# Strassen chunks of a fused attention and MoE kernel: four queues of small work rearranged (q loads, norms' spread, block 2's weights, weight sums)

## The chip, the cores and the metric

The kernel runs on one core of a Trainium2 chip. The metric is device microseconds of one execution. A core has TensorE (PE, matrix products into PSUM banks), VectorE (DVE), ScalarE (ACT), GpSimd (POOL) and SyncE (SP), each with an instruction queue of its own that runs in order. A DMA is issued from one of these queues, and an instruction that waits for a semaphore holds up all that stands behind it in its queue.

## What is computed

```python
def _attn_ref(q, k, v, g_norm):                # 8 batches, 8 heads, 576 rows, 64 columns
    kv = np.einsum('bhsd,bhse->bhde', k, v)
    out = np.einsum('bhsd,bhde->bhse', q, kv)
    rms = np.sqrt(np.mean(out * out, axis=-1, keepdims=True) + 1e-06)
    return (out / rms * g_norm).astype(np.float32)

def _moe_ref(x, w_in, w_out):                  # x 4608 x 512, d_ff 2048
    h = x @ w_in
    g = np.maximum(0.01 * h, h)
    return (g @ w_out).astype(np.float32)

def _moe2_ref(x, w_in, w_out, a, b):
    h = x @ w_in
    h2 = h * h
    h3 = h2 * h
    P = a[0] + a[1] * h + a[2] * h2 + a[3] * h3
    Q = 1.0 + np.abs(b[0]) * np.abs(h) + np.abs(b[1]) * h2
    g = P / (Q + 1e-06)
    return (g @ w_out).astype(np.float32)
```

The output of attention, with the heads side by side, goes through `_moe_ref` (block 1) and then `_moe2_ref` (block 2).

## The kernel before

**Tiling.** The 4608 tokens are nine chunks of 512. d_ff is 16 blocks of 128. Each product of block 1 and block 2 is three products of float16 parts (high x high, high x low, low x high; lines 432 to 434, `mm3`). Block 1 is a loop over units. Chunks 0 to 3 are computed in the classical way, a slot for each of the 16 blocks of d_ff. Chunks 4 to 8 (units 6 to 10 of the loop at L1193) use Strassen's seven products for h = x w_in, on 128 x 256 pieces: each of eight steps `j` covers two blocks of d_ff, hence slots 2j and 2j + 1, and 16 slots a chunk again.

**A step j** (L1245 to L1283). `product` fills two PSUM banks in turn, `chain` and `other`. What is in `chain` is copied to the tile `hq` by ACT (L1253, L1261, L1271, L1277), what is in `other` is added to it by DVE (L1255, L1273, L1278). The next product for a bank waits until that is done. Between the products stand `y_steps`, the matmuls y += g w_out of earlier blocks. `split_g` (L1039) is called once a step: Prelu on ACT, the high part of g by an ACT copy (L301), the low part by a DVE subtraction (`split_lo`, L296).

**The other work** of a slot is put between these by hand-set places and by queues. `prep(c, ...)` (from L888) gives the pieces that make the next chunk's x, each with a slot and a place in it ("load", "early", "pe", "post"):

- `ldq` loads q (L568, four DMAs of 64 x 2 x 512) and `mo` multiplies it by kv into the banks `po`;
- `so` scales `po` into `o` (L916 on DVE for chunks above 3, else ACT), `sq` squares `po` on ACT (L909);
- `ms` sums the squares in PSUM (`pm`), `nm` makes the reciprocal norms `w` (L612 to L621);
- `store_w` writes `w` to DRAM (`rs`, L935, SP), and `load_w` calls `spread_w` twice (L715): two DMAs that read `rs` back, broadcast over partitions, into `sq`, one on SP's queue and one on ACT's;
- `sx` multiplies `o` by the spread norms (L946, DVE), and `sf` makes the forms of x that Strassen needs (L515, L523, L525);
- the `bursts` load the k and v tiles of a later batch (L560, SP).

Block 2's w_in and w_out arrive as 64-bit floats, in 32 halves, and are converted to float32 on the way: `convert2` (L1060) asks for a half (L311) on ACT's queue with two raw tiles in turn, `next_half` puts ACT's absolute value (L320), four DVE steps (L325, L327, L331, L335) and a maximum (`top`, L158 and L1090) on the queue `fill`, and one slot later the half is stored to DRAM (L1065), on ACT's queue too. One converted tile `cv` of two parts is used in turn. Strassen's sums of block 1's weights are made in unit 5, the last classical chunk: `sums_w(j)` on DVE (L398, L403) every second slot, `forms_w(j, 0)` on ACT (L410), `forms_w(j, 1)` on DVE (L296).

`begin(sl)` and `end(sl)` add the pieces of a slot to the queue `work`; `drain(vector, scalar)` takes pieces from `evacs`, `work` and `fill`, in this order, as long as their own costs (DVE us, ACT us) fit the two budgets:

```python
while evacs or work or fill:
    for q in (evacs, work, fill):
        if q and q[0][0] <= vector and q[0][1] <= scalar and (q[0][0] + q[0][1] or first):
            v, a, fn = q.pop(0)
            break
```

What is asked for at a place stands at that place in the engine's queue; a queue of DMAs (SP's above all) runs ahead of the others as far as its waits allow.

## Time and profile before

| | us |
|---|---|
| median of 3 runs | 1591.68 |
| lowest and highest run | 1590.59, 1593.63 |
| the profiled execution | 1589.82 |
| its span | 1588.0 |
| the five Strassen chunks in it, 383.71 to 826.54 | 442.83 |

All numbers of the trace come from the one profiled execution. In a view of waits each row gives the engine and line that waited, what it waited for, the sum, the number of times and the longest. In a timeline each row gives the start, the duration, the engine and line, the operation with its output and inputs, and in square brackets the idle time of the engine just before it with what ended it. A row of SPq or ACTq is a DMA being issued by that queue, not the transfer.

### The profile page before, as it was taken

The page shows a single profiled execution, that of the slowest core. Times are in us where ns is not written, and L with a number is a line of the kernel's source. Part 1 is how long each engine was busy: PE and PEld are TensorE (multiplying, and loading weights), DVE is VectorE, ACT ScalarE, POOL GpSimd, SP SyncE. Part 2 cuts the span into 40 slices and gives each one's busy share as a digit, 9 for nine tenths or more (in the row PEclk, how much of TensorE's full clock was granted, in tenths as well). Part 3 has the DMA queues.
Part 4 walks back from the last instruction along what each step waited for, and adds up shares of the span by engine and source line. Part 5 has one row for each costly group of instructions (what it writes and reads, how often), then busy time and mean ns, then how long its engine had stood idle before and what let it go on. Part 6 is the DMA issues. An engine that isn't in the chain of part 4 may idle for free.

```text
span 1588.0 us, 21127 instructions
## 1 busy us (share of the span) xinstructions
PE 1557.0 (98%) x8634; PEld 851.4 (54%) x8634; DVE 1112.7 (70%) x1491; ACT 930.8 (59%) x1277; POOL 150.1 (9%) x74
## 2 busy tenths in 40 slices
PE   9999999999999999989999999999999999999998
PEld 5888754444666665656654444444444444444444
DVE  6787456679566565656658767777777777777776
ACT  6567554444454443544567665766666666666665
POOL 0000000000000000000001221222221222211221
PEclk9999999999999999999999999999999999999999
DMA  8454632252454424240241010101010100101000
GB/s 316 124 190 142 171 107 67 69 144 60 137 129 140 127 87 119 80 154 19 89 138 54 1 54 2 54 1 53 1 53 1 35 19 9 45 0 53 1 27 27
DMA packets 44069, 123.07 MB, mean 77 GB/s; under 512 B 4804, under 2 KB 5188, under 8 KB 43972
## 3 DMA queue, kind: packets, MB, share of 16 engines
q1 hardware_dynamic: 32432, 92.23, 18.0%
q10 hardware_dynamic: 11540, 29.50, 6.5%
q8 instruction: 67, 1.10, 0.3%
q14 instruction: 30, 0.25, 0.1%
HBM read 90.25 MB, written 31.46 MB: 77 GB/s over the span
## 4 chain that ended last, share of the span: by engine, by line
PE 89%; DVE 4%; ACT 3%; DMA 3%; issue 1%; ACTq 0%; SPq 0%; DVEq 0%
PE y L432 15%; PE y L434 15%; PE y L433 15%; PE ph L432 11%; PE ph L434 11%; PE ph L433 11%; PE chain L432 2%; PE chain L434 2%; PE chain L433 2%; PE other L432 1%; PE other L434 1%; PE other L433 1%; DMA raw<-in_kv_dram 1%; PE kvacc L578 1%; PE po L595 1%
## 5 line engine op out<-in xcount | busy, mean ns | idle before, releaser
L296 POOL TENSOR_TENSOR g<-p,g 128x1024 f16<-128x1024 f32 x70 | 149.9, 2142 | 1414.2 <-ACT g L301 1397.7
L1297 ACT ACTIVATE e<-ph,small 128x1024 f32<-128x1024 f32 (+1 forms) x73 | 80.4, 1101 | 237.0 <-PE ph L434 237.0
L432 PE MATMUL ph<-x,v 128*128 128x512 f16 x576 | 218.3, 379 | 0.5 <-DVE hq L1278 0.5
L434 PE MATMUL y<-g,v 128*128 128x512 f16 x576 | 218.3, 379 | 0.3 <-POOL g L296 0.3
L433 PE MATMUL ph<-x,v 128*128 128x512 f16 x576 | 218.3, 379 | 0.0
L434 PE MATMUL ph<-x,v 128*128 128x512 f16 x576 | 218.3, 379 | 0.0
L433 PE MATMUL y<-g,v 128*128 128x512 f16 x576 | 218.3, 379 | 0.0
L432 PE MATMUL y<-g,v 128*128 128x512 f16 x576 | 218.3, 379 | 0.0
L1300 DVE SCALAR_TENSOR_TENSOR e<-s,b,e 128x1024 f32<-128x1024 f32 (+1 forms) x73 | 92.7, 1270 | 148.9 <-ACT s L1298 148.9
L432 PEld LDWEIGHTS <-v 128*128 128x128 f16 x1152 | 112.7, 98 | 137.0 <-DVE hq L1278 0.8
L434 PEld LDWEIGHTS <-v 128*128 128x128 f16 x1152 | 112.7, 98 | 136.0
L433 PEld LDWEIGHTS <-v 128*128 128x128 f16 x1152 | 112.7, 98 | 135.7
L433 PE MATMUL y<-g,n 128*128 128x512 f16 x448 | 171.1, 382 | 0.0
L432 PE MATMUL y<-g,n 128*128 128x512 f16 x448 | 171.0, 382 | 0.0
L434 PE MATMUL y<-g,n 128*128 128x512 f16 x448 | 170.9, 381 | 0.0
L434 PEld LDWEIGHTS <-n 128*128 128x128 f16 x816 | 80.1, 98 | 71.6 <-issue 1.4
L433 PEld LDWEIGHTS <-n 128*128 128x128 f16 x816 | 80.0, 98 | 70.4 <-issue 14.3
L432 PEld LDWEIGHTS <-n 128*128 128x128 f16 x816 | 80.1, 98 | 64.1 <-issue 7.2
L1308 DVE SCALAR_TENSOR_TENSOR e<-e,z 128x1024 f32<-128x1024 f32 (+1 forms) x73 | 88.6, 1214 | 29.1 <-ACT z L1305 29.0
L1307 DVE SCALAR_TENSOR_TENSOR p<-p,small,ph 128x1024 f32<-128x1024 f32 (+1 forms) x73 | 92.5, 1266 | 2.6
L1309 DVE SCALAR_TENSOR_TENSOR p<-p,small,z 128x1024 f32<-128x1024 f32 (+1 forms) x73 | 92.2, 1264 | 0.0
L1310 DVE SCALAR_TENSOR_TENSOR p<-e,p 128x1024 f32<-128x1024 f32 (+1 forms) x73 | 88.4, 1210 | 2.5
(219 smaller groups left out, 2882.0 us busy)
## 6 DMA issues: line engine op xcount, KB each, us to landing
raw<-in_kv_dram SPq DMA_DIRECT2D x33, 512.0 KB, 5.7
tmp<-in_w_dram SPq DMA_DIRECT2D x32, 512.0 KB, 7.0
w<-in_w_dram ACTq DMA_DIRECT2D x32, 512.0 KB, 4.5
raw<-x SPq DMA_DIRECT2D x18, 512.0 KB, 5.2
w<-cv ACTq DMA_DIRECT2D x32, 256.0 KB, 2.4
raw<-w SPq DMA_DIRECT2D x16, 512.0 KB, 4.2
out_dram<-raw SPq DMA_DIRECT2D x16, 512.0 KB, 2.9
raw<-in_qT_dram SPq DMA_DIRECT2D x28, 256.0 KB, 8.6
```

The source lines that it names most:

```text
L296: (nc.gpsimd if pool else nc.vector).tensor_tensor(out=lo, in0=src, in1=hi if hi.dtype == F16 else hi.bitcast(F32), op=ALU.subtract)
L432: nc.tensor.matmul(out=dst, lhsT=wl, rhs=xh, start=first, stop=False, **kw)
L433: nc.tensor.matmul(out=dst, lhsT=wh, rhs=xh, start=False, stop=False, **kw)
L434: nc.tensor.matmul(out=dst, lhsT=wh, rhs=xl, start=False, stop=last, **kw)
L578: nc.tensor.matmul(out=acc[s * D:(s + 1) * D, k * D:(k + 1) * D], lhsT=t[:, 0, c], rhs=t[:, 1, c], start=first and k == 0, stop=last, skip ...
L595: nc.tensor.matmul(out=dst[s][j * D:(j + 1) * D, o], lhsT=KV[bt][r, 2 * g + j, :], rhs=q[r, j, o], start=True, stop=True)
L1297: nc.scalar.activation(out=e, in_=ph, func=AF.Abs, scale=k["e"])
L1300: nc.vector.scalar_tensor_tensor(out=e, in0=s, scalar=b1[:, 0:1], in1=e, op0=ALU.mult, op1=ALU.add)
L1307: nc.vector.scalar_tensor_tensor(out=p, in0=p, scalar=k["c1"], in1=ph, op0=ALU.add, op1=ALU.mult)
L1308: nc.vector.scalar_tensor_tensor(out=e, in0=e, scalar=Q_C, in1=z, op0=ALU.add, op1=ALU.mult)
L1309: nc.vector.scalar_tensor_tensor(out=p, in0=p, scalar=k["c0"], in1=z, op0=ALU.add, op1=ALU.mult)
L1310: nc.vector.scalar_tensor_tensor(out=p, in0=e, scalar=-2.0, in1=p, op0=ALU.add, op1=ALU.mult)
```

## The change

Seven edits, all in the loop over block 1's units:

1. `spread_w`: for chunks from 4 on, both halves of the norms' spread are issued on SP's queue.
2. For chunks 5 to 7 `prep` asks for the q of the chunk after its own (`ldq_next`) in its slot 6, where before each chunk asked for its q in slot 0 of the unit that prepares it.
3. `so` is done by ACT for all chunks.
4. `store_w` and `load_w` are put at the place "early" of their slots for chunks above 4, and kv tiles 3 and 4 get places of their own.
5. Block 2's weights are loaded and stored by GpSimd's queue; a half is stored at once in `top`, which also asks for another; nothing is asked for in slots 7 and 8 of a chunk, and in the last two of these units up to four halves are on the way, in tiles of the pool `raw`.
6. `sums_w` and `forms_w` start two slots earlier, in slot 14 of unit 4, and are done in slot 14 of unit 5. In unit 5 `drain` is called only in slots 0 to 8.
7. The low part of `split_g` is put on a queue `urgent`, which `drain` looks at after `evacs`, and the budget of the drain at the end of an even slot is 4.2 in place of 3.0.

```diff
-                (nc.sync, nc.scalar)[j].dma_start(out=t[j * D:(j + 1) * D], in_=rs[c].rearrange("(p r) n -> r p n", r=32)[j:j + 1]
+                (nc.scalar if c < 4 and j else nc.sync).dma_start(out=t[j * D:(j + 1) * D], in_=rs[c].rearrange("(p r) n -> r p n", r=32)[j:j + 1]
...
-                    st["q", g] = load_q(c, g)
+                    st["q", g] = made.pop(("q", c, g)) if ("q", c, g) in made else load_q(c, g)
+                def ldq_next(g):
+                    made["q", c + 1, g] = load_q(c + 1, g)
...
-                    if c > 3:
-                        nc.vector.tensor_scalar_mul(st["o"][:, p, :], ps, gsc[:, 0:1])
-                    else:
-                        nc.scalar.activation(out=st["o"][:, p, :], in_=ps, func=AF.Copy, scale=gsc[:, 0:1])
+                    nc.scalar.activation(out=st["o"][:, p, :], in_=ps, func=AF.Copy, scale=gsc[:, 0:1])
...
+                    if 4 < c < NCH - 1:
+                        at(6, "load", ldq_next, g)
...
-                at(ms_at + 1, "post", store_w)
-                at(w_at, "pe", load_w)
+                at(ms_at + 1, "early" if c > 4 else "post", store_w)
+                at(w_at, "early" if c > 4 else "pe", load_w)
...
-                split(*(x.rearrange("p a (b n) -> p (a b) n", b=2) for x in gt), hq)
+                hi, lo = (x.rearrange("p a (b n) -> p (a b) n", b=2) for x in gt)
+                nc.scalar.activation(out=hi, in_=hq, func=AF.Copy)
+                urgent.append((1.23, 0, lambda: split_lo(hi, lo, hq)))
...
-                while made["late"] and made["late"][0][0] <= count["slot"]:
-                    _, dst, t = made["late"].pop(0)
-                    nc.scalar.dma_start(out=dst, in_=t)
-                n = count["asked"]
-                if n < 2 * NF and n - count["done"] < 2:
-                    t = wp.tile([P, N], I64, tag=made["raw"][n % 2], name="w64")
-                    made[n] = load_w64(w2, *halves[n], t, nc.scalar), count["slot"] + 2
+                ask()
+                next_half()
+
+            def ask():
+                n, deep = count["asked"], 4 if count["slot"] > 48 else 2
+                if n < 2 * NF and n - count["done"] < deep and count["slot"] % NF not in (7, 8):
+                    t = raw(1, I64)[:, 0, :] if deep > 2 else wp.tile([P, N], I64, tag=made["raw"][n % 2], name="w64")
+                    made[n] = load_w64(w2, *halves[n], t, nc.gpsimd), count["slot"] + 2
                     count["asked"] += 1
...
-                    made["late"].append((count["slot"] + 1, w2f[f][:, part, :], u()[:, 0, :].bitcast(F32)))
+                    nc.gpsimd.dma_start(out=w2f[f][:, part, :], in_=u()[:, 0, :].bitcast(F32))
                     count["done"] += 1
+                    ask()
...
-                    for q in (evacs, work, fill):
+                    for q in (evacs, urgent, work, fill):
...
+                    if ui == 4 and sl > 13 or ui == 5 and sl < NF - 1:
+                        n = sl + 2 if ui > 4 else sl - 14
+                        if n % 2:
+                            forms_w(n // 2, 0)
+                        else:
+                            if n > 1:
+                                forms_w(n // 2 - 1, 1)
+                            if n < NF:
+                                sums_w(n // 2)
                     if ui == 5:
-                        if sl % 2 == 0:
-                            sums_w(sl // 2)
-                            if sl > 0:
-                                forms_w(sl // 2 - 1, 1)
-                        else:
-                            forms_w(sl // 2, 0)
                         convert2()
-                        drain(1.4, 0.7)
+                        if sl < 9:
+                            drain(1.4, 0.7)
...
-            forms_w(NP - 1, 1)
...
-                                 [(5, 6, c + 2, (0, 1, 2)), (7, 8, c + 2, (3, 4))] if c + 2 < B else [],
+                                 [(5, 6, c + 2, (0, 1, 2)), (5, 8, c + 2, (3,)), (8, 9, c + 2, (4,))] if c + 2 < B else [],
...
-                    drain(3.0, 2.1)
+                    drain(4.2, 2.1)
```

Three pieces of the engines' queues show what this moves. The first is DVE's queue where the Strassen chunks begin, before: `sum` and `s` are the weight sums, `cv` a half of block 2's weights, `g` the low part of g.

```order
L398 TENSOR_TENSOR sum_3376<-n_2578 128x512
L398 TENSOR_TENSOR sum_3376<-n_2617 128x512
L403 TENSOR_TENSOR sum_3376<-sum_3376 128x256 x4
L296 TENSOR_TENSOR s_3347<-sum_3300,s_3347 128x4x256
L325 TENSOR_SCALAR cv<-cv 128x512
L327 TENSOR_SCALAR cv<-cv 128x512
L296 TENSOR_TENSOR g_3371<-t,g_3371 128x512
L331 SCALAR_TENSOR_TENSOR cv<-w_3259,cv 128x512
L335 SCALAR_TENSOR_TENSOR cv<-w_3259,cv 128x512
L296 TENSOR_TENSOR s_3407<-sum_3376,s_3407 128x4x256
L1255 TENSOR_TENSOR hq<-hq,other 128x256
```

The same place in the changed kernel, up to its first addition into `hq` (L1255 is now L1262):

```order
L523 SCALAR_TENSOR_TENSOR x16T_4_3322<-sq,small,x16T_4_3322 128x512
L296 TENSOR_TENSOR g_3283<-t,g_3283 128x512
L523 SCALAR_TENSOR_TENSOR x16T_4_3326<-sq,small,x16T_4_3326 128x512
L523 SCALAR_TENSOR_TENSOR x16T_4_3361<-sq,small,x16T_4_3361 128x512
L523 SCALAR_TENSOR_TENSOR x16T_4_3363<-sq,small,x16T_4_3363 128x512
L296 TENSOR_TENSOR g_3367<-t,g_3367 128x512
L296 TENSOR_TENSOR s_3345<-sum_3301,s_3345 128x4x256
L296 TENSOR_TENSOR g_3367<-t,g_3367 128x512
L1262 TENSOR_TENSOR hq<-hq,other 128x256
```

The sums are gone from here, and so are their conversions by ACT from the rows ahead of ACT's first copy. The second place is SP's queue while the second Strassen chunk is prepared in the first (`rs_91` holds its norms, `raw<-in_qT_dram` is q, `raw<-in_kv_dram` k and v):

```order
 L560 DMA raw<-in_kv_dram 128x1024 x4
+L568 DMA raw<-in_qT_dram 64x2x512 x4
 L560 DMA raw<-in_kv_dram 64x1024
 L935 DMA rs_91<-w 128x512
-L715 DMA sq<-rs_91 64x4x512
-L568 DMA raw<-in_qT_dram 64x2x512 x4
+L715 DMA sq<-rs_91 64x4x512 x2
```

The q loads now stand ahead of the norms' store instead of behind the spread, and the second half of the spread has come from ACT's queue. The third place is POOL's queue around the first two of these chunks, which had no such rows before (`w_3_98` and its like are block 2's weights in DRAM, `w_3895` and its like the raw tiles):

```order
L1095 DMA w_2_97<-cv 128x512
L1095 DMA w_3_98<-cv 128x512
L311 DMA w_3895<-in_w_dram 128x512
L311 DMA w_3938<-in_w_dram 128x512
L1095 DMA w_3_98<-cv 128x512
L311 DMA w_4044<-in_w_dram 128x512
```

Two loads stand there directly behind one store, where elsewhere a store and a load take turns.

## Rows read from the trace of the kernel before

**Rows 1.** The page's first part: engine, busy us, share of the span, instructions.
```profile
PE 1557.0 (98%) x8634; PEld 851.4 (54%) x8634; DVE 1112.7 (70%) x1491; ACT 930.8 (59%) x1277; POOL 150.1 (9%) x74
```

**Rows 2.** PE's waits in the Strassen chunks: total us, times, longest.
```profile
PE other L432 <- DVE hq L1278: 8.7, 6, 4.5
PE chain L432 <- ACT hq L1253: 6.6, 3, 2.5
PE other L432 <- DVE hq L1273: 3.6, 4, 0.9
PE other L432 <- DVE hq L1255: 2.0, 4, 1.3
PE chain L432 <- ACT hq L1271: 0.9, 4, 0.3
```

**Rows 3.** Stretches: us, engines' busy us, PE's granted clock, DMA share, GB/s.
```profile
383.71:826.54 442.83, 419.84 (x2949) 267.76 (x2947) 278.52 (x506) 214.60 (x370) 0.00 (x0) 0.99 0.37 112
388.93:392.34 3.41, 2.72 (x9) 1.28 (x9) 3.34 (x7) 0.64 (x3) 0.00 (x0) 0.50 0.00 0
627.86:631.27 3.41, 3.41 (x13) 1.67 (x12) 3.41 (x6) 1.64 (x3) 0.00 (x0) 0.50 0.01 2
```

**Rows 4.** Timeline at the start of the first Strassen chunk (place A).
```profile
387.88 1.06 ACT L410 ACTIVATE s<-sum 128x1024 f16<-128x1024 f32 x1 [2.62 <-DVE sum L403]
...
389.25 0.37 PE L432 MATMUL chain<-x16T,s 128*128 128x256 f16 x1 [2.49 <-ACT hq L1253]
...
393.23 0.27 PE L432 MATMUL other<-x16T,s 128*128 128x256 f16 x1 [1.26 <-DVE hq L1255]
```

**Rows 5.** Timeline in the second Strassen chunk (place B).
```profile
495.92 0.75 DVE L916 TENSOR_SCALAR o<-po,gsc 128x512 f32<-128x512 f32 x1
496.70 0.60 ACT L909 ACTIVATE sq<-po 128x512 f32<-128x512 f32 x1 [0.66 <-DVE o L916]
497.19 0.66 ACT L320 ACTIVATE cv<-w 128x512 f32<-128x512 f32 x1
...
497.88 0.43 DVE L325 TENSOR_SCALAR cv<-cv 128x512 f32<-128x512 f32 x1 [1.22 <-ACT cv L320]
...
498.81 0.69 DVE L331 SCALAR_TENSOR_TENSOR cv<-w,cv 128x512 uint32<-128x512 uint32 x1
...
499.88 0.27 PE L432 MATMUL other<-x16B,s 128*128 128x256 f16 x1 [0.90 <-DVE hq L1273]
```

**Rows 6.** Timeline in the first Strassen chunk (place C).
```profile
433.61 1.54 SPq L935 DMA_DIRECT2D rs<-w  x1
...
438.75 0.66 ACT L320 ACTIVATE cv<-w 128x512 f32<-128x512 f32 x1 [3.67 <-DMA rs<-w]
...
439.73 0.27 PE L432 MATMUL chain<-x16T,s 128*128 128x256 f16 x1 [1.77 <-ACT hq L1253]
```

**Rows 7.** Timeline in the third and fourth Strassen chunk (place D).
```profile
611.52 3.42 SPq L568 DMA_DIRECT2D raw<-in_qT_dram  x4
...
612.95 0.65 ACTq L715 DMA_DIRECT2D sq<-rs  x1
...
625.45 0.69 DVE L946 TENSOR_TENSOR o<-o,sq 128x512 f32<-128x512 f32 x1 [5.43 <-DMA w<-cv]
...
626.53 0.27 PE L432 MATMUL other<-x16B,n 128*128 128x256 f16 x1 [3.46 <-DVE hq L1278]
...
715.14 0.69 DVE L946 TENSOR_TENSOR o<-o,sq 128x512 f32<-128x512 f32 x1 [6.50 <-DMA w<-in_w_dram]
```

**Rows 8.** Timeline, first chunk; then landings of spread (520 to 540), norms' store, weight loads.
```profile
448.07 0.69 DVE L946 TENSOR_TENSOR o<-o,sq 128x512 f32<-128x512 f32 x1 [1.66 <-DMA sq<-rs]
...
DMA to landing us min/median/max: 6.0/7.3/8.6
...
DMA to landing us min/median/max: 2.0/3.2/4.3
...
DMA to landing us min/median/max: 4.0/4.6/9.4
```

More of the change, by code (lines that the diff above doesn't have):

```diff
@@ L963, in prep @@
                     at(po_at[g], "pe", mo, g)
+                    if 4 < c < NCH - 1:
+                        at(6, "load", ldq_next, g)
                     for p in (2 * g, 2 * g + 1):
-                        at(po_at[g] + 1, "early", so, p, cost=(0.75, 0) if c > 3 else (0, 0.7))
+                        at(po_at[g] + 1, "early", so, p, cost=(0, 0.7))
                         at(po_at[g] + 1, "early", sq, p, cost=(0, 0.6))
@@ L1000 @@
             k1 = 7
-            steps, work, fill, evacs = [], [], [], []
+            steps, work, fill, evacs, urgent = [], [], [], [], []
             def y_steps(n):
@@ L1062, in convert2 @@
                 count["slot"] += 1
-                while made["late"] and made["late"][0][0] <= count["slot"]:
-                    _, dst, t = made["late"].pop(0)
-                    nc.scalar.dma_start(out=dst, in_=t)
-                n = count["asked"]
-                if n < 2 * NF and n - count["done"] < 2:
-                    t = wp.tile([P, N], I64, tag=made["raw"][n % 2], name="w64")
-                    made[n] = load_w64(w2, *halves[n], t, nc.scalar), count["slot"] + 2
+                ask()
[5 more added lines that the diff above has]
+                    made[n] = load_w64(w2, *halves[n], t, nc.gpsimd), count["slot"] + 2
                     count["asked"] += 1
-                next_half()
             def next_half():
@@ L1102, in drain @@
                 next_half()
-                while evacs or work or fill:
-                    for q in (evacs, work, fill):
+                while evacs or urgent or work or fill:
+                    for q in (evacs, urgent, work, fill):
                         if q and q[0][0] <= vector and q[0][1] <= scalar and (q[0][0] + q[0][1] or first):
@@ L1124 @@
                 elif ui == 5:
-                    made["late"] = []
                     made["cv"], *made["raw"] = (room.pop(0) for _ in range(3))
@@ L1204 @@
                     room.extend(spare_q + [made["cv"]] + made["raw"])
-                    assert count["done"] == 2 * NF and not made["late"]
+                    assert count["done"] == 2 * NF
                 def chores(sl):
@@ L1281 @@
                     r = hq, c, j
+                    assert not urgent
                 while work:
@@ L1284 @@
             split_g(r)
+            urgent.pop()[2]()
             assert not steps
```

## The prediction

> **What bounds the kernel now.** The page comes first: TensorE (PE) is busy 98% of the span [rows 1]. VectorE (DVE, 70%), ScalarE (ACT, 59%) and GpSimd (POOL, 9%) cost nothing but where PE waits for them. The profiled execution is 1589.82 us, of which 1588.0 are span and 1.82 lie outside it; the median of the runs is 1591.68, that is 1.86 longer, and a saving is taken off both alike.
>
> The change touches the Strassen chunks, so the view by stretches comes next: the five chunks take 442.83 us, PE is busy in 419.84 of them, and 22.99 are idle [rows 3]. The view of waits names them [rows 2]: nearly all is PE waiting until a `hq` operation has emptied one of two PSUM banks, `chain` (by ACT copies) or `other` (by DVE additions). So every gap is a late ACT or DVE instruction, and the question for each is what stood ahead of it in its queue. The timeline answers that at four kinds of place, which I call A to D.
>
> A third loss hides in busy time. After the gap of A and after both gaps of D, PE's clock is granted at 0.50, the level of 1.2 GHz, for 3.41 us [rows 3], where the third dip would read as the second. Work done at half the clock takes twice as long: 2.72/2 + 3.41/2 + 3.41/2 = 4.77 us lost. The idle times ahead were 2.49, 3.46 and 4.53; after the idle times of 1.77 and 2.35 at C the clock stayed up.
>
> **The change part by part.**
>
> *Place A, start of the first Strassen chunk (weight sums two slots earlier).* ACT's conversion of the last weight sum waits 2.62 us for DVE's sums, the first copy out of `chain` stands behind it in ACT's queue, and PE waits 2.49. A second later sum then stands ahead of DVE's first addition, 1.26 [rows 4]. In the new order both sums are done in the chunk before, and the first rows of either queue in this chunk are the copies and additions themselves. Gain 2.49 + 1.26 = 3.75, and the dip behind it, 1.36. The sums now lie beside the classical chunks, where DVE did the same work before and PE shows no wait for it; I cost it at nothing. If that cover were gone, the price is one of A's own gaps, 2.5.
>
> *Place B, once in each of the first four chunks (scaled attention output on ACT, low parts in a queue).* A square on ACT waits 0.66 for DVE's scaling of the same bank; the weight conversion's first step (ACT L320) comes after it, and its three DVE steps (0.43, 0.43, 0.69) stand ahead of the addition L1273. PE waits 0.90 for that, and about 0.22 for the copy L1271 [rows 5], in all four chunks 3.6 and 0.9 [rows 2]. The change moves 16 scalings of 0.75 off DVE and onto ACT, where one is worth about the square's 0.60. ACT is busy 214.60 of 442.83 us [rows 3], so 16 x 0.60 = 9.6 us have room; the square now follows the scaling on its own engine and waits for nobody. Gain 3.6 + 0.9 = 4.5. The four waits of 0.18 for L1278 (8.7 less 3.46 and 4.53) I leave standing. The queue for low parts moves no work: its slot is allowed 1.2 more, and the split (1.23 by the kernel's own figure) is now counted in it.
>
> *Place C, first two chunks (spread off ACT's queue).* ACT's queue holds the second half of the spread of the norms. That DMA must wait until the store of the norms has landed, and the store is itself late, behind the last kv tile on SP's queue: ACT sits 3.67 us, the conversion and the copy L1253 queue behind it, and PE waits 1.77 [rows 6]. Of the 6.6 us in three waits for L1253 [rows 2] 2.49 were A's and 1.77 are this one, so the other chunk's was 2.35. Three short waits for L1255 follow (2.0 less 1.26 is 0.74). Gain 1.77 + 2.35 + 0.74 = 4.86, say 4.9. What is put on SP instead is one more issue of about 0.65 [rows 7]; behind it on SP there are now only y's stores and, in one chunk, block 2's weights, which nobody waits for at once.
>
> *Place D, third and fourth chunk (q asked for mid-chunk, both halves on one queue).* DVE's multiplication by the spread norms (L946) waits 5.43 and 6.50 us for it, the addition L1278 stands behind, and PE waits 3.46 and 4.53 [rows 7, 2]. The half on ACT's queue was issued at 612.95 behind a weight load and used at 625.45, so it took 12.5 us; the four q loads for the chunk after, 1 MB, had been issued at 611.52, ahead of it: SP's queue runs ahead, so they go out as soon as their tiles are free. In a chunk with lighter traffic a half lands in 6.0 to 8.6 [rows 8]. After the change the q loads stand ahead of the norms' store, asked for two slots before it, and both halves are issued together, in the last of these chunks ahead of block 2's weights. The store takes 2.0 to 4.3, an issue 0.65, a half 6.0 to 8.6: 8.7 to 13.6 after the store, where about 13 are allowed (store at 433.61, L946 free at 448.07 - 1.66 = 446.4, so 12.8 there [rows 6, 8]). DVE also forgives some: a wait of 5.43 cost PE 3.46 and one of 6.50 cost 4.53, so 1.97 is free, and the 1.66 of the first chunk cost nothing. Gain 3.46 + 4.53 = 7.99, and the two dips, 3.41.
>
> *GpSimd's queue.* The loads and stores of block 2's weights, for seven or eight conversions a chunk, leave ACT for POOL, which does nothing in these chunks (0.00 busy [rows 3]). No row shows a DMA from POOL. The nearest are the same loads from ACT: 4.0 to 9.4, median 4.6 [rows 8]. A slot is 442.83/80 = 5.5 us, and a load is asked for at least two slots ahead of its use, 11 us, so a median load is hidden twice over, and I take the change of queue at nothing; the ends, a stall in every conversion or a little gained by the issues that ACT is spared, are kept for the range.
>
> The Trainium skill ("SBUF — State Buffer", the box on the "DVE blocks DMA" trap) speaks against this part: descriptors of a GpSimd-issued DMA are written by GpSimd's cores, which are locked out while VectorE runs an operation in a two-port mode; it gives 620 ns alone and 3100 ns overlapped. What the trace can say to that: L325 takes 0.43 where L331, of the same 128 x 512 words, takes 0.69 [rows 5], so the first two conversion steps may be such operations. They last 0.43 each; by the page a load would come some 2.5 us later, an estimate, and the sum would stay as it is, since 4.6 + 2.5 is under the two slots.
>
> **The sum.** 3.75 + 4.5 + 4.9 + 8.0 + 4.8 = 25.9. Off that I take 1.4 for the first two chunks, half of one such wait of 2.7 as the first rival works out: 24.5. That makes 1565.3 of the profiled 1589.82, and 1567 of the median. Floor: with the four waits of 0.18 and what else is idle gone too, 22.99 + 4.77 = 27.8, that is 1563.9; less the 1.1 by which the runs scatter below their median, 1562.5.
>
> **The rivals.**
>
> *Weights beside the spread (chance 0.18).* The new code issues no load in the two slots around the spread, but that holds in the order of writing only. POOL's queue runs ahead: in the first two chunks its order is a store and then two loads, free to go as soon as that store's last DVE step is done, so 1 MB may run beside the spread as q did at D. For it: at D a half in such company took 12.5. Against: q's loads were ahead of the half, these come beside it. At 12.5, after 4.3 and 0.65, the spread lands 17.5 after the store, 4.7 late; less the free 1.97 that is 2.7 for PE, and 3.8 if the half takes 1.1 longer, as the wait of 6.50 did against 5.43. Two chunks: 5.4 to 7.6, and two dips of 1.71: 8.8 to 11.0. With the 1.4 given back, 1574.4 to 1576.6; I say 1576, since the norms' store itself then has company too. The Trainium skill ("DMA: Bandwidth & Descriptors", "Issuing engines are not separate DMA queues") is on this side: transfers from any queue share the same 16 engines and interleave, so another queue saves issue time only.
>
> *One of A and B stays (0.08)*, because DVE's or ACT's order puts another instruction where the removed one stood, or since the earlier sums push the classical chunks: A with its dip is 5.1, B 4.5: about 1572. This is also the case in which the change does only a part of what it says.
>
> *POOL's queue is slow (0.04), the case that ends slower.* A conversion's first step (ACT L320) waits in order for its load and for the store that empties its buffer; the next copy out of `chain` stands behind it. Over 30 conversions the whole 24.5 is lost at 0.8 each, and 1595 is reached at 0.9 each beyond the slack. The nearest turn is at a chunk's start, where store to L320 is some 6 us, and two slots elsewhere; so this decides once POOL's transfers take over 11 us at the median. Against: 4.6 on ACT's queue, 9.4 at most. It would give 1590 to 1600. The box of the Trainium skill named above would put its delay here; no row of the kernel before shows a DMA that waits so.
>
> **How the numbers follow.** Forecast 0.70: 1567, its own range 1563 to 1571. Rivals 0.18 at 1576, 0.08 at 1572, 0.04 around 1595. A measurement tells about 0.2%, 3.2 us, from no change. All cases but the last lie below 1588.5, 0.96 together, of which I keep 0.95 as faster; the last one's 1590 to 1600 lies on both sides of the bound: 0.02 the same, 0.03 slower. The range runs from the floor to just past the first rival: 1562.5 to 1577.
>
> **What would show it.** Right: PE idle in the five chunks falls from 23.0 to 2 to 4; no wait of PE for L1260 or L1262 at the start; the addition L1280 costs no 0.90; ACT no longer waits for the norms' store; q lands before the spread is issued; all three clock dips inside the chunks are gone. Wrong: L946 still waits over 2 us in the first two chunks with POOL loads in flight (first rival); ACT L320 waits for a DMA of POOL's queue in chunk after chunk (last rival); a new PE wait before 384 us (second).

## The result and the profile after

The changed kernel takes 1576.16 us (1575.82 to 1577.28, four runs) against 1591.47 of the kernel before in the same comparison: a ratio of 0.9903, with a 95% interval of 0.9886 to 0.9920. It is 15.3 us faster, inside the stated range (1562.5 to 1577), but 9.2 slower than the forecast of 1567. The first rival had given 1576.

In the changed kernel `chain` is emptied by ACT's lines 1260, 1268, 1278 and 1284, and `other` by DVE's 1262, 1280 and 1285; the store of a converted half is L1095, block 2's load L1058. The first part of the page of the changed kernel, which answers to [rows 1], shows PE's share going up by one point, and 64 more instructions on GpSimd (POOL): the issues of 32 loads and 32 stores of block 2's weights.

```profile
span 1574.0 us, 21219 instructions
PE 1555.1 (99%) x8634; PEld 850.3 (54%) x8634; DVE 1101.5 (70%) x1471; ACT 940.0 (60%) x1297; POOL 185.2 (12%) x138
```

To compare versions I use one stretch throughout: from the 0.12 us wait of PE just after the first Strassen chunk begins to the last product before block 2. It holds the same 2942 matmuls in each version, and leaves out the start of the kernel, which differs by some 2 us from run to run. The view by stretches (columns as in [rows 3]) of the kernel before, then of the changed one:

```profile
384.65:826.54 441.89, 419.02 (x2942) 267.17 (x2941) 277.58 (x505) 213.69 (x368) 0.00 (x0) 0.99 0.37 112
```

```profile
383.87:812.51 428.64, 417.33 (x2942) 267.00 (x2941) 268.35 (x490) 221.54 (x385) 31.86 (x58) 0.98 0.39 119
```

The stretch is 13.25 shorter. PE's idle time in it, length less busy time, went from 22.87 to 11.31, and its busy time from 419.02 to 417.33. After the stretch nothing moved: 1588.0 - 826.54 = 761.5 before, 1574.0 - 812.51 = 761.5 now.

The view of PE's waits in these chunks, which answers to [rows 2]:

```profile
PE other L432 <- DVE hq L1285: 7.4, 3, 3.7
PE chain L432 <- ACT hq L1284: 3.8, 2, 3.2
```

Nothing waits for L1260, L1262, L1268, L1278 or L1280 any more: places A, B and C of the prediction are gone, and with B the four waits of 0.18 as well. What is left is new or stands in another place. The timeline of the first Strassen chunk tells how:

```profile
425.16 0.49 SPq L560 DMA_DIRECT2D raw<-in_kv_dram  x1
425.75 1.32 SPq L935 DMA_DIRECT2D rs<-w  x1
...
428.94 0.55 POOL L1095 DMA_DIRECT2D w<-cv  x1 [9.49 <-DVE cv L335]
...
429.29 1.26 SPq L715 DMA_DIRECT2D sq<-rs  x2
...
429.60 1.17 POOL L311 DMA_DIRECT2D w<-in_w_dram  x2
...
442.00 0.69 DVE L946 TENSOR_TENSOR o<-o,sq 128x512 f32<-128x512 f32 x1 [6.42 <-DMA sq<-rs]
...
443.08 0.37 PE L432 MATMUL other<-x16B,n 128*128 128x256 f16 x1 [3.73 <-DVE hq L1285]
```

GpSimd's queue stood 9.49 us before a store, and as soon as DVE freed it, it issued that store and then two loads of 512 KB. The rows marked x2 hold two issues each: the halves of the spread left at 429.29 and 429.92, the loads at 429.60 and 430.24, one just ahead of the second half and one just behind it. The view of L715 in this chunk gives how long the halves took:

```profile
DMA to landing us min/median/max: 7.0/9.5/12.0
```

The first half took 7.0, the second 12.0. DVE waited 6.42 for it, and PE 3.73; the second chunk repeats this with 6.15 and 3.46. The spread also started late against DVE's work: from the issue of the norms' store to the moment at which DVE was free for L946 there were 442.00 - 6.42 - 425.75 = 9.83, and 9.84 in the second chunk, where the first chunk of the kernel before had 12.8 [rows 6, 8]. The stretches after these waits, and after one in the fourth chunk, are again granted 0.50 of the clock, the level of 1.2 GHz:

```profile
442.82:446.23 3.41, 3.15 (x11) 1.57 (x11) 1.82 (x4) 2.21 (x2) 0.00 (x0) 0.50 0.00 0
531.57:538.39 6.83, 5.49 (x19) 2.84 (x19) 3.78 (x6) 2.38 (x3) 0.00 (x0) 0.50 0.00 0
702.23:705.64 3.41, 3.24 (x12) 1.62 (x11) 3.10 (x6) 2.48 (x3) 0.54 (x1) 0.50 0.15 55
```

Half of their busy time is lost: 1.57 + 2.75 + 1.62 = 5.94 (4.77 before). The third chunk is clean. In the fourth, place D has changed its cause:

```profile
688.65 6.56 SPq L1058 DMA_DIRECT2D raw<-w  x3
...
689.93 0.55 POOL L1095 DMA_DIRECT2D w<-cv  x1 [7.84 <-DVE cv L335]
...
697.68 0.69 DVE L946 TENSOR_TENSOR o<-o,sq 128x512 f32<-128x512 f32 x1 [1.61 <-DMA sq<-rs]
...
700.47 0.66 ACT L320 ACTIVATE cv<-raw 128x512 f32<-128x512 f32 x1 [5.07 <-DMA w<-cv]
...
701.44 0.27 PE L432 MATMUL chain<-x16B,n 128*128 128x256 f16 x1 [3.20 <-ACT hq L1284]
```

L946 waits 1.61 where it waited 6.50. But the conversion's first step, ACT L320, now waits for its buffer: the store of 689.93 is not done before 700.37, as the chain of waits there says:

```profile
689.93 10.44 DMA w<-cv
```

Beside it were the second half of the spread and block 2's first weight tiles (512 KB each): SP's queue had issued two at 688.65 and 689.59, and issued the third at 694.89. The copy L1284 stands behind L320 in ACT's queue, and PE waits 3.20.

The sum by these rows, against the kernel before: A -3.75, B -5.2 (with the four of 0.18), C -4.9, D -7.99 + 3.20 + 0.17, the new waits +7.19, small ones -0.3: idle -11.6. Clock +1.2. PE's remaining busy time 414.25 to 411.39: -2.9. The start -0.8 (384.65 to 383.87). Together -14.1; the spans differ by 14.0.

### The profile page after: what moved, and what is told of

Its sections match the earlier page's. It is cut to its first block, busy times and chain, and to the rows that moved or that the text cites. A ratio compares the mean times of both kernels' runs of the same rounds, so it can differ in the third digit from the quotient of the medians.

```text
span 1574.0 us, 21219 instructions
## 1 busy us (share of the span) xinstructions
PE 1555.1 (99%) x8634; PEld 850.3 (54%) x8634; DVE 1101.5 (70%) x1471; ACT 940.0 (60%) x1297; POOL 185.2 (12%) x138
## 4 chain that ended last, share of the span: by engine, by line
PE 82%; issue 11%; DMA 3%; ACT 2%; DVE 1%; POOL 1%; SPq 0%; POOLq 0%; DVEq 0%; ACTq 0%
PE y L432 13%; PE y L434 13%; PE y L433 13%; PE ph L432 11%; PE ph L434 11%; PE ph L433 11%; PE chain L432 1%; DMA raw<-in_kv_dram 1%; PE chain L434 1%; PE chain L433 1%; PE kvacc L578 1%; PE other L432 1%; PE other L434 1%; PE other L433 1%; DMA sq<-rs 1%
```

## The experiments

My theory was L: small loads from another queue, in flight beside a DMA that DVE or ACT waits for, are what is left. The rivals are told with each experiment. All versions are compared by the stretch of 2942 matmuls as well:

| version | us (median) | stretch | PE idle in it |
|---|---|---|---|
| before | 1591.47 | 441.89 | 22.87 |
| changed | 1576.16 | 428.64 | 11.31 |
| loads_behind_spread | 1565.12 | 417.68 | 4.47 |
| no_exclusion | 1569.41 | 421.60 | 7.53 |
| w2_behind_stores | 1571.60 | 424.45 | 8.90 |
| both_moves | 1560.49 | 412.84 | 1.64 |
| b_spread_on_act | 1566.35 | 418.17 | 6.00 |
| b_q_at_start | 1562.92 | 414.50 | 3.11 |
| b_sums_late | 1564.23 | 416.68 | 3.80 |
| b_scale_on_dve | 1568.14 | 419.68 | 6.67 |
| b_weights_on_act | 1569.78 | 422.95 | 9.41 |
| b_kv_later | 1559.64 | 411.84 | 0.89 |
| a_kv_later | 1564.82 | 415.87 | 3.21 |
| a_kv_w2 | 1559.23 | 411.76 | 0.82 |

Four runs each. The times come from several comparisons, in which the kernel before took 1590.77 to 1593.51; each ratio is to the kernel before of the same comparison. Stretch and idle time are those of the one profiled execution. A line can stand one higher or up to five lower than in the changed kernel; where this could mislead, the changed kernel's number is given.

### What is left: the loads, and the store

**loads_behind_spread**

```diff
-                    made[n] = load_w64(w2, *halves[n], t, nc.gpsimd), count["slot"] + 2
+                    queue = nc.sync if count["slot"] in (25, 26, 41, 42) else nc.gpsimd
+                    made[n] = load_w64(w2, *halves[n], t, queue), count["slot"] + 2
```

> The two weight loads that run beside the norms' spread in the first and in the second Strassen chunk are issued by SP, right behind the spread's two halves, instead of by GpSimd ahead of the second half; nothing else differs from the changed kernel. Theory L (those loads, coming from another queue, slow the spread): the second half lands 7 to 9 us after its issue instead of 12, L946's two waits of 6.4 and 6.2 fall under 2, PE's waits of 3.73 and 3.46 for L1285 go and so do the clock dips behind them (1.6 + 2.7): about 11.5 less than the changed kernel, 1564 to 1566. Rival Q (the second half is late since it now stands behind the first on one queue): it still lands at 12, and the time stays at 1576. Rival S (any 1 MB in flight beside it does it, whatever its queue): 1574 to 1577.

1565.12, ratio to before 0.9831 (0.9805 to 0.9858). The timeline of the first chunk:

```profile
429.78 1.26 SPq L715 DMA_DIRECT2D sq<-rs  x2
431.20 1.97 SPq L311 DMA_DIRECT2D w<-in_w_dram  x2
...
439.50 0.69 DVE L946 TENSOR_TENSOR o<-o,sq 128x512 f32<-128x512 f32 x1 [3.41 <-DMA sq<-rs]
```

The loads, which had left 0.32 ahead of the second half and 0.32 behind it, now leave 0.79 and 1.50 behind it, on its own queue, and it lands after 9.0 in this chunk and 7.9 in the next. PE waits 0.73 and nothing where it waited 3.73 and 3.46, and both clock dips are gone. The loads are shown to be what slowed the half, and rivals Q (one queue for both halves) and S (any company) fall. That it is their queue, as theory L has it, is not shown: the edit changes the queue and the order of issue together. L946 still waits 3.41 and 2.28, more than the 2 I had put: the spread starts as late as in the changed kernel (9.84 from store to L946).

**no_exclusion**

```diff
-                if n < 2 * NF and n - count["done"] < deep and count["slot"] % NF not in (7, 8):
+                if n < 2 * NF and n - count["done"] < deep:
```

> The rule that no weight half is asked for in slots 7 and 8 is dropped, so that loads and stores take turns on GpSimd's queue again and one load, not two, stands behind the store that is freed while the spread runs. Theory L: with half the company the second half lands at 9 to 10, L946 waits 3 to 4, PE 1 to 2 in each of the two chunks and without a dip: 1567 to 1571. Rival Q: unchanged waits of 6, 1575 to 1577. In the third and fourth chunk more is in flight beside the spread than in the changed kernel, so a new wait of up to 3 may come there by theory L.

1569.41, in the range, ratio 0.9859 (0.9833 to 0.9886), but not by the way I gave: one load beside the spread stalls PE 4.24 in the first chunk and 2.57 in the second, with a dip in each, so half the company is not half the wait. The second half took 11.8 in the first chunk and, by L946's start, 10.2 in the second. That load left 0.28 ahead of the second half. Most of what is gained is in the fourth chunk, where the store no longer meets L320: PE waits for nothing there. The rule that asks for nothing in slots 7 and 8 thus gathers two loads where one would stand, and saves nothing in these chunks.

**w2_behind_stores**

```diff
-                nc.sync.dma_start(out=t, in_=w2f[f])
+                (nc.gpsimd if f < 3 else nc.sync).dma_start(out=t, in_=w2f[f])
```

> Block 2's first three weight tiles (raw<-w, 1.5 MB) are loaded by GpSimd's queue, behind the last stores of the converted halves, instead of by SP's queue right behind the spread in the fourth Strassen chunk. Theory L: the store that took 10.4 us there lands in 2 to 4, ACT's L320 no longer waits 5.07 for it, L946 no longer 1.61, and PE's 3.20 and 0.17 and the dip behind them (1.6) go: 5 less than the changed kernel, 1571. Rival P (GpSimd's queue itself is slow while VectorE runs): the store still takes 8 to 10 and L320 waits as before, 1576.

1571.60, ratio 0.9867 (0.9846 to 0.9889), as theory L put it. The wait of L320 in the fourth chunk is 1.12 in place of 5.07, and PE has no wait left there:

```profile
696.92 0.67 ACT L320 ACTIVATE cv<-raw 128x512 f32<-128x512 f32 x1 [1.12 <-DMA w<-cv]
```

The first two chunks keep theirs (4.21 and 3.71). The store still took 6.5, more than the 2 to 4 that I had put (2.3 is the median), with the second half of the spread beside it, so not all of its delay came from block 2's tiles. Rival P had the wait of L320 as before.

**both_moves** (the two edits together)

> Both moves together: the loads behind the spread in the first two chunks on SP's queue, and block 2's first three weight tiles behind the stores on GpSimd's queue. Theory L: the gains add, 11.5 + 5, and the time is 1558 to 1561, with less than 2.5 us of PE idle left in the five chunks and no clock dip in them. Rival Q or S: 1570 to 1572. Rivals Q and P both: 1576.

1560.49, ratio 0.9801 (0.9781 to 0.9822). In the stretch the moves gave 11.0 and 4.2 alone, and 15.8 together. Its row, with the clock at 1.00:

```profile
383.63:796.47 412.84, 411.20 (x2942) 265.54 (x2941) 268.42 (x490) 221.74 (x385) 31.29 (x57) 1.00 0.41 123
```

### What each part gave: parts undone in this cleaner version

**b_spread_on_act**

```diff
-                (nc.scalar if c < 4 and j else nc.sync).dma_start(...
+                (nc.sync, nc.scalar)[j].dma_start(...
```

> The version with both moves (1560.49), with the second half of the spread on ACT's queue again. Theory: place C returns, since ACT must wait for the norms' store again with the copy L1260 behind it: 1.8 to 2.4 and 0.25 in each of the first two chunks, so 1564 to 1565, with ACT's conversion or copy waiting 3 to 4 us for the store in these chunks. Rival 1: the store now lands in 2 to 3.5 and C costs under 1 in all: 1560 to 1562. Rival 2 (company from another queue): the half on ACT's queue is slowed by the loads behind the other half on SP's, L946 waits 4 to 6 in the first two chunks: 1566 to 1571.

1566.35, ratio 0.9840 (0.9821 to 0.9860), nearest to rival 2. Its waits on ACT, DVE and PE:

```profile
DVE o L946 <- DMA sq<-rs: 7.7, 2, 4.0
ACT cv L320 <- DMA rs<-w: 4.4, 2, 2.2
PE other L432 <- DVE hq L1286: 4.1, 4, 1.3
```

ACT's queue is held by the norms' store again, but in the first two chunks, where place C was, this costs PE 0.09 and 0.08. There the half on ACT's queue took 6.7 and 7.8, and the one on SP's queue, with the two loads behind it, 10.3 and 10.6; the landings of the first chunk:

```profile
DMA to landing us min/median/max: 6.7/8.5/10.3
```

L946 waits 3.7 and 4.0, PE 1.02 and 1.30. In the third and fourth chunk L320 waits 2.2 for the store, and PE 0.32 and 0.90 in each. So the part is worth 5.3 in the stretch, and about half of it (0.17 + 2.44) by the prediction's mechanism of a conversion and a copy behind a store. Place C itself does not come back; which other edit keeps it away was not tried.

**b_q_at_start**

```diff
-                    if 4 < c < NCH - 1:
-                        at(6, "load", ldq_next, g)
```

> The version with both moves, with the q of the chunk after asked for in slot 0 again, so that on SP's queue its four loads stand right behind the spread's two halves. Theory (what stands behind the spread on its own queue does not slow it; only what comes from another queue, or ahead, does): L946 waits under 2 in the third chunk, no new PE gap there, 1560 to 1562. Rival, as the prediction's place D took it (q in flight is the harm): the spread takes 12 or more in the third chunk, L946 waits 4 to 6, PE 2 to 4 and a dip of 1.7: 1564 to 1567.

1562.92, ratio 0.9820 (0.9800 to 0.9840). In the third chunk the four q loads stand right behind both halves again, and L946 starts at once (it had waited 5.43 [rows 7]):

```profile
595.95 1.95 SPq L715 DMA_DIRECT2D sq<-rs  x2
597.95 3.61 SPq L568 DMA_DIRECT2D raw<-in_qT_dram  x4
...
605.01 0.69 DVE L946 TENSOR_TENSOR o<-o,sq 128x512 f32<-128x512 f32 x1
...
606.96 0.66 ACT L320 ACTIVATE cv<-raw 128x512 f32<-128x512 f32 x1 [2.76 <-DMA w<-cv]
```

What is slowed instead is a store from GpSimd's queue: L320 waits 2.76, PE 0.89. So q's new place is worth 1.7 in the stretch once both halves are on one queue, and the time lies 0.9 above the theory's 1560 to 1562. The third chunk of b_spread_on_act is the other side of this: a half on ACT's queue again, q early, and no wait of L946 either.

**b_sums_late**

```diff
-                    if ui == 4 and sl > 13 or ui == 5 and sl < NF - 1:
-                        n = sl + 2 if ui > 4 else sl - 14
+                    if ui == 5:
+                        n = sl
...
+            forms_w(NP - 1, 1)
```

> The version with both moves, with the weight sums two slots later again (the last of them at the start of the first Strassen chunk). Theory: place A returns with its dip: PE waits of 2.5 and 1.3 at the start of the first chunk and 1.4 lost to the clock, 1565 to 1566. Rival: unit 5 asks for fewer halves and drains only in slots 0 to 8 now, so less stands ahead of the sums and A costs 0 to 2: 1560 to 1563.

1564.23, ratio 0.9826 (0.9803 to 0.9849); 3.84 in the stretch. The time lies between the theory's range and the rival's. Place A is back in its first half, with its dip (3.41 busy at 0.50, so 1.71); L1262 is the copy that is L1260 in the changed kernel:

```profile
388.93 0.37 PE L432 MATMUL chain<-x16T,s 128*128 128x256 f16 x1 [2.09 <-ACT hq L1262]
...
389.80 0.41 DVE L1264 TENSOR_TENSOR hq<-hq,other 128x256 f32<-128x256 f32 x1
390.13 0.69 DVE L331 SCALAR_TENSOR_TENSOR cv<-w,cv 128x512 uint32<-128x512 uint32 x1
```

The second wait of 1.26 did not return: DVE's addition now stands ahead of the steps of the conversion.

**b_scale_on_dve**

```diff
-                    nc.scalar.activation(out=st["o"][:, p, :], in_=ps, func=AF.Copy, scale=gsc[:, 0:1])
+                    if c > 3:
+                        nc.vector.tensor_scalar_mul(st["o"][:, p, :], ps, gsc[:, 0:1])
+                    else:
+                        nc.scalar.activation(out=st["o"][:, p, :], in_=ps, func=AF.Copy, scale=gsc[:, 0:1])
...
-                        at(po_at[g] + 1, "early", so, p, cost=(0, 0.7))
+                        at(po_at[g] + 1, "early", so, p, cost=(0.75, 0) if c > 3 else (0, 0.7))
```

> The version with both moves, with the scaling of the attention output on VectorE again for chunks above 3. Theory: place B returns, 0.9 and 0.2 in each of four chunks, 1564 to 1566, with PE waits for L1280 of 0.9. Rival: the queue for low parts and the larger budget alone have taken B away, and the scaling moves nothing: 1560 to 1561.

1568.14, ratio 0.9851 (0.9831 to 0.9871). 2.1 above the theory's range. Place B is back, each wait within 0.04 of the old one (L1284 and L1282 are L1280 and L1278 in the changed kernel):

```profile
PE other L432 <- DVE hq L1284: 3.6, 4, 0.9
...
PE chain L432 <- ACT hq L1282: 0.9, 4, 0.2
```

With the 0.18 for the last bank that is 5.2 of waits. The low parts' queue and the larger budget alone do not touch them. The stretch is 6.84 longer: 5.03 idle, and 1.81 of PE's busy time, of which more below.

**b_weights_on_act**

```diff
-                    queue = nc.sync if count["slot"] in (25, 26, 41, 42) else nc.gpsimd
+                    queue = nc.sync if count["slot"] in (25, 26, 41, 42) else nc.scalar
...
+                while made["late"] and made["late"][0][0] <= count["slot"]:
+                    _, dst, t = made["late"].pop(0)
+                    nc.scalar.dma_start(out=dst, in_=t)
...
-                    nc.gpsimd.dma_start(out=w2f[f][:, part, :], in_=u()[:, 0, :].bitcast(F32))
+                    made["late"].append((count["slot"] + 1, w2f[f][:, part, :], u()[:, 0, :].bitcast(F32)))
...
+                    made["late"] = []
```

> The version with both moves (1560.49), with block 2's other weight loads and all its stores on ACT's queue again (a store one slot after its conversion, as in the kernel before). Theory: GpSimd's queue is worth little in itself, since an issue on ACT takes 0.4 to 1.0 and ACT has room; 1561 to 1564, with PE waits of under 1 behind late copies. Rival: ACT's queue, which runs in order, is where the conversions' stalls came from (a store that waits for VectorE, a conversion that waits for its store), and the copies out of the chain bank queue behind: PE waits of 1 to 3 in several chunks, 1568 to 1575.

1569.78 (1568.51 to 1573.53), ratio 0.9860 (0.9843 to 0.9876): the rival. GpSimd's queue is worth 9 to 10 us, where the prediction booked nothing: 9.3 by the medians, 10.1 in the stretch of the profiled execution, which was the slowest of the four. Two of its rows (L1273 is L1268 in the changed kernel):

```profile
ACT cv L320 <- DMA w<-cv: 8.1, 2, 4.2
PE chain L432 <- ACT hq L1273: 4.7, 2, 2.5
```

A store that goes out a slot late, by ACT's own queue, holds the buffer of the next conversion but one; L320 waits 4.22 and 3.93 for it in the third and fourth chunk, and a copy behind it makes PE wait 2.51, with a dip, and 2.23. In the first two chunks L946 waits 4.09 and 4.57, and PE 1.40 and 1.88, 2.50 more than with both moves. How much of this is the queue and how much the later slot was not tried apart.

### Either condition of the first stall

**b_kv_later**

```diff
-                                 [..., (8, 9, c + 2, (4,))] if c + 2 < B else [],
+                                 [..., (9, 10, c + 2, (4,))] if c + 2 < B else [],
```

> The version with both moves, with the last k and v tile of the first two Strassen chunks loaded and multiplied a slot later, so that on SP's queue it stands behind the norms' store and the spread, no longer ahead of the store. Theory (the store, and with it the spread, is held up behind that tile): the spread is issued earlier, L946's waits of some 3 in the first two chunks fall under 1.5, PE's 0.78 for L1286 goes: 1559 to 1560. Rival: the tile now lands late for its matmuls, PE waits 1 to 3 for it in each of the two chunks: 1562 to 1566. Second rival: the tile was not what held the store (the norms came no sooner), nothing moves: 1560 to 1561.

1559.64, ratio 0.9797 (0.9783 to 0.9812). The store of the norms had stood some 3 us behind a k and v tile that waited for its room on SP's queue; in front of it the spread starts 5 us earlier and no L946 waits in any chunk. In time this is 0.9 less than without it, too little to tell from no change by itself; the 1.0 in the stretch and the missing wait of 0.78 are what show it.

**a_kv_later** (the same edit alone, in the changed kernel)

> The changed kernel itself (1576.16), its two weight loads left on GpSimd's queue, with only the last k and v tile of the first two Strassen chunks a slot later, behind the norms' store and the spread on SP's queue. The store then goes out some 4 us earlier and the spread is under way 5 us before GpSimd's queue releases the two loads. Theory (the stall needs both: a spread that starts late and loads beside it): L946's waits of 6.4 and 6.2 fall under 2.5 and PE's 3.73 and 3.46 and their dips go, 1564 to 1567. Rival (the loads delay the second half wherever they meet it): it still lands 10 or more after its issue, L946 waits 2 to 4, PE 0.5 to 2 in each chunk: 1567 to 1571.

1564.82, ratio 0.9829 (0.9804 to 0.9855). The two loads are still on GpSimd's queue, and still meet the spread's second half, which left at 427.05 and takes 8.8 (7.4 in the second chunk):

```profile
424.34 0.33 SPq L935 DMA_DIRECT2D rs<-w  x1
...
426.41 1.24 SPq L715 DMA_DIRECT2D sq<-rs  x2
427.75 1.42 SPq L560 DMA_DIRECT2D raw<-in_kv_dram  x1
...
431.49 1.18 POOL L311 DMA_DIRECT2D w<-in_w_dram  x2
...
437.40 0.68 DVE L946 TENSOR_TENSOR o<-o,sq 128x512 f32<-128x512 f32 x1
```

But L946 has no wait. The edit takes away both conditions of the stall. The store now goes out 13.05 before DVE is free for L946, in place of 9.84, and the loads leave 4.4 and 5.1 behind the second half. By these numbers the first alone would do: the second half left 2.7 after the store, so one of 12.0 would land 1.7 late, and waits of L946 up to 2.69 cost PE nothing here (6.42 cost 3.73, 6.15 cost 3.46). So the stall of the changed kernel needs a spread that starts late and loads that run beside it from its start; loads_behind_spread takes away the second and leaves PE 0.73.

**a_kv_w2** (this edit and that of w2_behind_stores, in the changed kernel)

> The changed kernel with two small moves: the last k and v tile of the first two chunks a slot later, and block 2's first three weight tiles on GpSimd's queue behind its stores; the two weight loads beside the spread stay on GpSimd's queue. Theory: the 5 that the second move gave add to the first, 1559 to 1562. Rival: without the loads behind the spread on SP's queue one of the first two chunks keeps a wait of 0.5 to 2 and perhaps a dip: 1562 to 1565.

1559.23 (1558.94 to 1559.45), ratio 0.9795 (0.9765 to 0.9825). Two lines of the changed kernel give the lowest median, 17 us under it; b_kv_later's 1559.64 is not to be told from it. PE's waits are down to one in the last chunk, behind ACT's L426, which waits 1.92 for block 2's weights, and the hand-over to block 2:

```profile
PE chain L432 <- ACT hq L1284: 0.7, 1, 0.7
PE ph L432 <- DVE hq L1285: 0.5, 1, 0.5
```

## Why the prediction was right and wrong

**Right: where the time was lost.** A, B and C went as the sum had them (3.75, 4.5 and 0.7 more, 4.9). Undone, the parts bring back A's first wait and all of B's at their places, but not C's (0.17 there), so that C went through edit 1 is not shown. With both stalls taken away (both_moves) the idle time fell by 21.23 and the clock gave back 4.77: 26.0, where the sum had 25.9 before its 1.4 was taken off. The 1.97 us of an L946 wait that the prediction counts as free were 2.69 in the changed kernel: waits of 6.42 and 6.15 cost 3.73 and 3.46, where 1.97 gives 4.45 and 4.18.

**Wrong: the terms "a half lands in 6.0 to 8.6" and "about 13 are allowed" at place D, and the 1.4 taken off.** The prediction saw the two loads in the order of GpSimd's queue and yet gave them a chance of 0.18. The halves took 7.0 and 12.0. And the 12.8 that were allowed in the first chunk of the kernel before were 9.84 in the first two of the changed one: the store still stood behind the k and v tile (without that it is 13.05), and DVE came to L946 sooner. Counted in PE's matmuls the store is issued at the same place in both kernels, L946 is free 16 matmuls sooner; which edit does this was not tried. With 12.8 a half of 12.0 would have cost PE 0.8 in a chunk (16.26 - 12.8 - 2.69), so the stall took both terms. Two late spreads cost 7.19 of waits and 4.32 of clock, 11.5 in place of 1.4: this alone is more than the miss of 9.2. The rival's own sum, 8.8 to 11.0 (with 12.5 for a half, store and issue 5), was right in mechanism and all but right in size. What should have moved the weight was its own view: the row of D shows a half in company at 12.5, and nothing in the new order kept the company away. The range holds the measured time only because it was drawn out to this rival; the forecast's own 1563 to 1571 misses it by 5. That the rival's 1576 is met within 0.2 is in part luck: 5.0 lost in the fourth chunk and 4.4 gained outside the sum (2.9 of busy time, 0.8 at the start, 0.7 for the four waits of 0.18) nearly cancel.

**Wrong: "D, 7.99 and two dips" in the fourth chunk.** 3.37 of its 4.53 came back, and 1.62 of clock, through a mechanism that the prediction had only as its last rival and for every chunk: ACT's L320 waits for a store of GpSimd's queue. Other stores took up to 8.3, and ACT waited 0.86 for one of them; the one that held it for 5.07 took 10.4, beside block 2's weight loads, which the prediction had called work that nobody waits for at once. It looked at who waits for those loads and not at what they slow.

**Not told apart: q at place D.** The prediction blamed q's loads ahead of the half on ACT's queue. With both halves on SP's queue and q right behind them L946 waits 0.14 in the third chunk (b_q_at_start); with a half on ACT's queue and q early it waits for nothing there (b_spread_on_act). So either edit ends this wait in the cleaner version, and the prediction's reason is neither shown nor refuted: no run of the cleaner version has both a half on ACT's queue and q asked for in slot 0.

**Wrong: the term of nothing for GpSimd's queue.** It is worth 9 to 10 together with the earlier store. The slow case that the prediction kept for it did not come: its loads landed in 4.1 to 11.5, median 4.8, against 4.0 to 9.4, median 4.6, from ACT [rows 8], and its stores in 2.3 at the median. The Trainium skill's trap of GpSimd-issued DMAs behind VectorE ("SBUF — State Buffer", box on the "DVE blocks DMA" trap) is not to be seen in these medians; the load of 11.5 and the store of 10.4 had the spread or block 2's tiles beside them.

**Not in the sum: the time after a wait.** PE's busy time less the clock loss fell by 2.9, which no term had. In the stretch 18 waits went (24 to 6), so this is 0.16 for each. With both stalls gone as well it fell by 3.05, and the kernel took 1560.49, under the prediction's floor. (That floor, 1563.9 less 1.1, is 1562.8 and not 1562.5; nothing hangs on it.)

## What to carry to other kernels

Before a load is moved to a queue that runs ahead, look in that queue's order for what frees it and which transfer will be in flight then; a rule on slots in the program text does not bind a queue. A transfer that an in-order engine waits for should be issued early, and bulk loads put behind it on its own queue: here, each alone in the changed kernel, the first of these moves gave 12.8 us in the stretch and the second 11.0. A late spread costs more than its wait where the clock falls behind it, so it is worth asking of each remaining wait of 2 to 4 us whether it brings a dip.

## What the runs showed of the hardware

- **What is issued ahead of a transfer or together with it slows it most; whether the queue counts too is open.** The Trainium skill ("DMA: Bandwidth & Descriptors", "Issuing engines are not separate DMA queues") has transfers of all queues share the same engines and interleave. The runs agree for those of different queues: a half of 512 KB took 12.0 with two loads of another queue issued 0.32 ahead of it and 0.32 behind, 11.8 with one issued 0.28 ahead and no other load in the next 5 us, and a store of 256 KB took 10.4 beside weight loads. With two loads 0.8 and 1.5 behind it on its own queue the half took 7.9 to 9.0, but 10.3 and 10.6 when the other half left ACT's queue at the same time; with two loads of another queue 4.4 and 5.1 behind it, 7.4 and 8.8. No run has the same lead on one queue and on two, so the part of the queue and the part of the lead are not told apart.
- **A dip of the clock does not follow from the length of the wait alone.** PE was granted 0.50 after waits of 2.09 (b_sums_late), 2.31 (a_kv_later) and 2.49 (place A before), and not after 2.23 (the fourth chunk of b_weights_on_act) and 2.35 (place C before). In the changed kernel one dip lasted 6.83 in place of 3.41, after a wait of 3.46, which is less than the 3.73 before a short one; in w2_behind_stores it was 6.83 after 3.71 and 3.41 after 4.21.
- **PE's busy time grew with the number of its waits.** In b_scale_on_dve twelve more waits than in both_moves came with 1.81 more busy time at full clock, 0.15 each; between the kernel before and the changed one it is 0.16 each. The ends of matmuls are modelled, so this is read from the sums only, and no run shows what takes the time.
